# Expert work in one clump behind a slot's own pieces, and token sums that begin two pieces later

## The chip, the cores and the metric

The kernel runs on one core of one Trainium2 chip. The metric is the device time of the slowest core, here the only one, in microseconds. Engines are named as in the profile: PE is TensorE (PEld its weight loads), DVE is VectorE, ACT is ScalarE, POOL is GpSimd, SP issues DMAs. Three runs of the kernel before took 2274.03, 2276.77 and 2281.79 us.

## The reference

Three stages follow each other, all in float32:

```
for t in range(768):                                  # 4 batches x 8 heads, state 48x48
    y[t]  = q[t] @ state
    state = state + beta[t] * outer(k[t], v[t] - k[t] @ state)   # k normalised
x = y as 3072 tokens x 384
P = exp(x @ w_gate); 8 rounds of row and column scaling           # 3072 x 8
x = sum over 8 experts of P[:, e] * (relu(x @ w1[e]) @ w2[e])      # 384 -> 1024 -> 384
out = gelu_sigmoid(x @ w_in) @ w_out                               # 384 -> 2048 -> 384
```

## The kernel before

**Two phases.** First the recurrence runs chunk by chunk, and beside it, on the same engines, the first of the eight experts (`expert0`), the gates and the conversion of the finished tokens. Then come 72 units: 56 for experts 1 to 7 (28 pairs of an expert and a quarter of its hidden columns, for each half of the tokens) and 16 for the MLP. Each unit forms 15 products of sums of token blocks with sums of weight blocks (a fast matrix multiplication, `SCHEME`), turns them into hidden values `h`, and multiplies those by the second weights (`po`).

**The recurrence.** 24 chunks (`u`) of 64 time steps. `Attention.chain` does a chunk in four steps, one matmul group each: `ks` (what the state holds for the keys), `up` (the solved update), `sp` (the new state), `y` (the output). ks is taken from PSUM by DVE (`r`, L356), and up waits for r. Each step yields, and the main loop (L731 to L750) then calls `slot`, so there are 96 slots. What stands in a slot is issued behind that step, and every engine works in the order of issue.

**A slot's own pieces.** `Attention.prep` prepares four chunks at a time (a group), cut into pieces that yield 1.0 or 0.5. The tables `PIECES` and `FIRST` (L29, L32) say how many of them each of a group's 16 slots takes. In order they are: eight gram pieces (`gram`: 16 matmuls `pg` in the trace, which DVE takes from PSUM in three instructions, `am` L187 and twice `x` L200; beside them POOL squares keys, DVE sums the squares, `ss` L127, and works out the step weights in eight small instructions, L141 to L149, and POOL makes the masks `bm`, L167, that the next grams' evictions read); two copies; a transposition on DVE; 30 substitution steps of two DVE instructions each (`lt` L276, `ln` L280), every one of which needs the one before; a transposition `ta` on DVE (L298); and products of 32-row blocks (`pz`, `px`, 64 matmuls each in the trace) with copies by ACT and one more transposition (`tt`, L324). Slots 0 to 2 of a group hold the grams (4, 2, 2), slots 5 to 12 the substitution, slots 13 to 15 the products.

**Expert items.** `expert0` yields after three matmuls: a third of a hidden block (`ph`, 128x256, three such items make one block, which ACT and then DVE take as `h`, L627 and L628) or half a second product (`po`, 128x384). `slot` spreads them: `expert(n / (k + 1) * step)` ahead of each piece and `expert(n / (k + 1))` behind the last, with n about 4.7 items a slot from slot 10 on.

**Turned tokens and gates.** At the second slot of a chunk (behind up), one expert item is issued and then the chunk before is transposed (`xt`, three matmuls, L402) and converted by `emit_x`: ACT writes the high part, DVE the low part (`xb`, L477), ACT the copy that goes to memory (L523). Two chunks make the 256 tokens of an `expert0`. Behind sp the gates' logits (`pl`, nine matmuls) are formed, behind y they are turned (`pt`), in even chunks. All this stands ahead of the slot's own pieces.

**PSUM.** pg, pz, px, xt, pl and pt share one pool of two buffers (`psg`); ks, up, sp and y have two of their own, ph two, po two.

**Token sums.** `sums(i, hf)` (L545) loads three token blocks (`braw`, L567, one buffer) and forms 15 sums of them with POOL; `put` splits a sum in a high part (ACT, `bo` L557) and a low part (POOL, L551) and stores both (L562). `sums(1, 0)` and `sums(1, 1)` make the MLP's tokens in units 29 and later and 57 and later, one step of the generator at certain products (L1108). Their first step behind the loads is a `put` of the loaded blocks themselves.

Of the kernel before, what the change touches and what calls it, by code (L numbers as in the profile page):

```python
# [34 lines left out]
LAG = 10  # L35
# [5 lines left out]
class Attention:  # L41
# [129 lines left out]
    def gram(self, u, planes, h0, n, pool=None):  # L171


        nc, x, j, bm = self.nc, self.X[u // 2 % 4], u % 2, self.bm.get(u)
        hs = slice(h0, h0 + n)
        where, tag = pool or (self.psg, "g")
        ps = where.tile([128, n, len(planes), 64], F32, tag=tag, name="pg")
        for h in range(n):
            for b in range(2):
                dr = slice(64 * b, 64 * b + D)  # L180
                nc.tensor.matmul(
                    ps[64 * (1 - b):64 * (1 - b) + 64, h], x[dr, 0, j, h0 + h],
                    x[dr, planes[0] * (1 + b):planes[-1] * (1 + b) + 1:1 + b, j, h0 + h], start=True, stop=True)
        m = 8 * (u % 4) + h0

        def take():
            nc.vector.tensor_tensor(out=self.am[:, m:m + n], in0=ps[:, :, 0], in1=self.bm[u][:, hs], op=ALU.mult)  # L187

        if pool in self.early:
            return take  # L190
        if planes[0] == 0:
            take()
        if planes[-1] == 1:
            for b in range(2):
                p = slice(64 * (1 - b), 64 * (1 - b) + 64)
                m = x[p, 1 + b, j, hs]
                if u < 8:
                    nc.scalar.copy(out=m, in_=ps[p, :, len(planes) - 1])
                else:
                    nc.vector.tensor_tensor(out=m, in0=ps[p, :, len(planes) - 1], in1=bm[p, hs], op=ALU.mult)  # L200
# [7 lines left out]
    def prep(self, g):  # L208

        nc, am, tt = self.nc, self.am, self.tt  # L210
        w, u = 2 * g, 4 * g
# [60 lines left out]
        for jj in range(1, 31):  # L272
# [16 lines left out]
            if jj == (15 if g == 0 else 22) and g < NG - 1:  # L289
                step = self.weights(*((2, 3) if g == 0 else (w + 2,)))  # L290
# [10 lines left out]
        zs = ta  # L301

        def pz(m0, n):
            ps = self.psg.tile([128, n, 32], F32, tag="g", name="pz")
            for m in range(n):
                for q in (0, 64):
                    nc.tensor.matmul(ps[q + 32:q + 64, m], am[q:q + 32, m0 + m, 32:64],
                                     ta[q:q + 32, m0 + m], start=True, stop=True, tile_position=(q, q + 32))
            for q in (0, 64):
                nc.scalar.copy(out=zs[q + 32:q + 64, m0:m0 + n], in_=ps[q + 32:q + 64])  # L310

        def px(m0, n):
            ps = self.psg.tile([128, n, 32], F32, tag="g", name="px")
            for m in range(n):
                for q in (0, 64):
                    nc.tensor.matmul(ps[q:q + 32, m], zs[q + 32:q + 64, m0 + m],
                                     tt[q + 32:q + 64, m0 + m, 32:64], start=True, stop=True,
                                     tile_position=(q + 32, q))
            for q in (0, 64):
                nc.scalar.copy(out=tt[q:q + 32, m0:m0 + n, 32:64], in_=ps[q:q + 32])  # L320
# [121 lines left out]
def kernel(  # L442
# [32 lines left out]
    def split(dst_hi, dst_lo, src, eng=nc.vector):  # L475
        nc.scalar.copy(out=dst_hi, in_=src)  # L476
        eng.tensor_tensor(out=dst_lo, in0=src, in1=dst_hi.bitcast(F32), op=ALU.subtract)  # L477
# [12 lines left out]
    A = Attention(tc, actx, ident, X, kq, kw, vw, bu, psg)  # L490
# [39 lines left out]
    def emit_x(u, xt):  # L530
        n, c = u // 2, 128 * (u % 2)
        if u % 2 == 0:
            xb[n] = ep.tile([128, 2, 3, 256], F32R, tag="xb", name="xb")
        t = xb[n]
        split(t[:, 0, :, c:c + 128], t[:, 1, :, c:c + 128], xt)
        keep(0, u, xt, ep.tile([128, 3, 128], F32, tag="x32", name="x32"))()
        if u % 2 == 1:
            r = n % 6
            nc.sync.dma_start(
                out=xd[n // 6][r // 2, :, :, :, 256 * (r % 2):256 * (r % 2) + 256].bitcast(F32), in_=xb[n].bitcast(F32))  # L540
# [4 lines left out]
    def sums(i, hf):  # L545


        g = nc.gpsimd

        def tt(o, a, b, op):  # L550
            g.tensor_tensor(out=o, in0=a, in1=b, op=op)  # L551

        def put(at, src):

            n = src.shape[1]
            o = bp.tile([128, 2, 3, 128], F32R, tag="o", name="bo", bufs=2)
            nc.scalar.copy(out=o[:, 0, 0:n], in_=src)  # L557
            yield
            tt(o[:, 1, 0:n], src, o[:, 0, 0:n].bitcast(F32), ALU.subtract)
            yield  # L560
            for k in range(n):
                nc.sync.dma_start(out=xs[i][hf][at + k, :, :, c:c + 128].bitcast(F32), in_=o[:, :, k].bitcast(F32))  # L562

        for c in range(0, 512, 128):
            raw = bp.tile([128, 3, 3, 128], F32, tag="raw", name="braw")
            for t in range(3):
                nc.sync.dma_start(out=raw[:, t], in_=xf[i][hf][t, :, :, c:c + 128])  # L567
            b = [[raw[:, t, d] for t in range(3)] for d in range(3)]
            v = bp.tile([128, 8, 128], F32, tag="v", name="bv")
            yield  # L570
            if i:
                yield from put(8, raw[:, 0:3, 0])
            tt(v[:, 4], b[2][1], b[2][2], ALU.subtract)
            tt(v[:, 5], b[0][0], b[1][0], ALU.add)
            tt(v[:, 0], b[1][2], v[:, 4], ALU.add)
            tt(v[:, 1], v[:, 4], b[0][2], ALU.subtract)
            yield
            if i:
                yield from put(11, raw[:, 1:3, 1])
            tt(v[:, 2], v[:, 5], b[1][1], ALU.subtract)  # L580
            tt(v[:, 3], v[:, 2], v[:, 1], ALU.subtract)
            tt(v[:, 3], v[:, 3], b[0][1], ALU.subtract)
            yield from put(0, v[:, 0:2])
            tt(v[:, 4], b[1][2], v[:, 5], ALU.subtract)
            tt(v[:, 5], b[1][1], b[1][0], ALU.subtract)
            tt(v[:, 5], v[:, 5], b[2][0], ALU.add)
            yield from put(2, v[:, 2:4])
            tt(v[:, 6], b[0][2], b[2][0], ALU.subtract)
            tt(v[:, 6], v[:, 6], b[2][2], ALU.add)
            tt(v[:, 7], zero, b[1][2], ALU.subtract)  # L590
            tt(v[:, 7], v[:, 7], b[2][0], ALU.subtract)
            yield from put(4, v[:, 4:6])
            if i:
                yield from put(13, raw[:, 0:2, 2])
            yield from put(6, v[:, 6:8])
            yield
# [94 lines left out]
    ex = []  # L691

    def expert_item():
        while ex:
            if next(ex[0], None) is not None:
                return True
            ex.pop(0)
        return False

    prep = chain.from_iterable(A.prep(g) for g in range(NG))  # L700
# [7 lines left out]
    done, due = 0, 0.0  # L708

    def expert(n):  # L710

        nonlocal done, due
        due += n
        while done < due and expert_item():
            done += 1

    def slot(t):

        n, k = rate * ITEMS[t % 16] if t >= LAG else 0, (PIECES if t > 15 else FIRST)[t % 16]
        if t == LAG:  # L720
            expert(BURST)
        i = 0
        while i < k:
            expert(n / (k + 1) * step[0])
            step[0] = next(prep, 1.0)
            i += step[0]
        expert(n / (k + 1))

    step = [1.0]
    build = sums(0, 0)  # L730
    for u in range(NU):  # L731
        for s, _ in enumerate(A.chain(u)):
            if s == 1 and u > 0:
                if 4 * u >= LAG:
                    due -= 1
                    expert(1)
                    done += expert_item()
                while u % 2 == 1 and len(ex) > 1:
                    done += expert_item()
                emit_x(u - 1, A.xt())  # L740
                if u % 2 == 0:
                    ex.append(expert0(u // 2 - 1))
            if s > 1 and u > 0 and u % 2 == 0:
                (logits if s == 2 else turn)(u // 2 - 1)
            slot(4 * u + s)
            while A.ready < u // 4:
                next(prep)
            next(ew, None)
            if u > 12:
                next(build, None)  # L750
        if u % 2 == 1 and u // 2 + 4 < 12:
            A.load_k(u // 2 + 4)
            A.load_x(u // 2 + 4)
# [300 lines left out]

    conv = convert64()
    building = [sums(0, 1)]
    later, turns = [], []
    load_w2(0)
# [8 lines left out]
    for j in range(len(units) + 1):  # L1067
# [3 lines left out]
        for k in range(len(SCHEME)):  # L1071
# [20 lines left out]
            if turns and turns[0][0] <= now:  # L1092
                u = turns.pop(0)[1]
# [75 lines left out]
```

## Time and profile before

| | |
|---|---|
| median of 3 runs | 2276.77 us |
| profiled execution: its time, its span | 2275.14 us, 2273.4 us |
| mean granted TensorE clock | 0.974 |
| busy: PE, DVE, ACT, POOL | 95%, 67%, 47%, 50% |
| start of the recurrence's last y (L389) in the span | 503.45 us |

The profile is one execution. Times in rows are microseconds from the span's start. A timeline row gives start, duration, engine, line, operation, tile written and tiles read, shape and count, and in brackets how long the engine was idle before and what ended it. A row of the waits gives who waited for whom, the total, how often, and the longest. A row of the stretches gives for each engine busy microseconds and instructions, then the granted clock (1.00 is 2.4 GHz, 0.50 is 1.2 GHz) and the DMAs' share and rate. Matmul ends are modelled, so lengths of matmul work are read from start to start.

### The profile page before, as it was taken

The numbers are of one execution on the slowest core, as the hardware profiler recorded it, in microseconds if no ns is written. First come the engines' busy times: TensorE is split into PE (matmuls) and PEld (weight loads), VectorE is DVE, ScalarE is ACT, GpSimd is POOL, SyncE is SP. The second block draws the span as 40 slices with busy tenths as digits, with TensorE's granted clock in tenths as the row PEclk, the third lists the DMA queues.
The fourth block names the chain that finished last, engine by engine and source line by source line (L and its number), as shares of the span: only waits on it lengthen the run. The fifth ranks groups of instructions, "written<-read, shape, count | busy, mean of one in ns | idle before, by whom it ended". The sixth has DMA issues, their size and how long they took to land. (4 is left out here: it accounts for less than half of the span.)

```text
span 2273.4 us, 40807 instructions
## 1 busy us (share of the span) xinstructions
PE 2161.1 (95%) x15663; PEld 1945.2 (86%) x15663; DVE 1520.3 (67%) x2754; ACT 1065.2 (47%) x2125; POOL 1128.3 (50%) x1326
## 2 busy tenths in 40 slices
PE   4499999998999999999999999999999999999999
PEld 4488888896989999999998989998989998888988
DVE  6666866626766677776666767777765556666675
ACT  2334344444444444444445444454554446555554
POOL 5511132224677766666652655565655334752333
PEclk8599999999999999999999999999999999999999
DMA  5223334238435343333358656556455366557231
GB/s 120 61 82 82 88 97 115 76 103 314 143 114 181 122 166 132 128 126 122 143 198 251 185 166 193 175 178 217 160 180 163 113 231 177 159 157 247 91 118 49
DMA packets 229155, 336.74 MB, mean 148 GB/s; under 512 B 15649, under 2 KB 192417, under 8 KB 224801
## 3 DMA queue, kind: packets, MB, share of 16 engines
q1 hardware_dynamic: 228240, 333.26, 45.6%
q8 instruction: 123, 2.02, 0.4%
q10 hardware_dynamic: 720, 0.89, 0.1%
q14 instruction: 72, 0.58, 0.1%
HBM read 204.58 MB, written 129.50 MB: 147 GB/s over the span
## 5 line engine op out<-in xcount | busy, mean ns | idle before, releaser
L481 PE MATMUL po<-w2c,h 128*128 128x384 f32 x1728 | 588.2, 340 | 0.0
L482 PE MATMUL po<-w2c,h 128*128 128x384 f32 x1728 | 586.4, 339 | 0.7 <-DVE h L982 0.7
L480 PE MATMUL po<-w2c,h 128*128 128x384 f32 x1728 | 580.1, 336 | 0.3 <-ACT h L980 0.2
L480 PE MATMUL c<-xt,w1c 128*128 128x512 f32 x1080 | 431.3, 399 | 19.8 <-DVE sg L979 10.5
L1037 POOL TENSOR_TENSOR acc<-acc,ye 128x384 f32<-128x384 f32 x252 | 263.0, 1044 | 374.9 <-ACT ye L1036 357.4
L482 PE MATMUL c<-xt,w1c 128*128 128x512 f32 x1080 | 430.6, 399 | 2.3 <-POOL w1c L477 2.3
L481 PE MATMUL c<-xt,w1c 128*128 128x512 f32 x1080 | 429.3, 398 | 0.0
L1014 DVE TENSOR_TENSOR o<-o,c 128x512 f32<-128x512 f32 x288 | 197.5, 686 | 255.9 <-PE c L482 232.1
L1039 DVE SCALAR_TENSOR_TENSOR acc<-po,P,acc 128x384 f32<-128x384 f32 x420 | 258.3, 615 | 153.0 <-PE po L482 150.5
L480 PEld LDWEIGHTS po<-w2c,h 128*128 128x128 f32 x1728 | 325.7, 188 | 40.3 <-ACT ye L1036 0.7
L481 PEld LDWEIGHTS po<-w2c,h 128*128 128x128 f32 x1728 | 324.7, 188 | 40.0
L482 PEld LDWEIGHTS po<-w2c,h 128*128 128x128 f32 x1728 | 325.8, 189 | 1.1 <-DVE h L982 1.1
L1036 ACT ACTIVATE ye<-po,P 128x384 f32<-128x384 f32 x252 | 146.9, 583 | 349.9 <-PE po L482 336.1
L480 PEld LDWEIGHTS c<-xt,w1c 128*128 128x128 f32 x1080 | 203.8, 189 | 50.9 <-DVE h L973 19.6
L482 PEld LDWEIGHTS c<-xt,w1c 128*128 128x128 f32 x1080 | 203.3, 188 | 47.8 <-POOL w1c L477 3.1
L481 PEld LDWEIGHTS c<-xt,w1c 128*128 128x128 f32 x1080 | 203.7, 189 | 9.0
L1007 ACT COPY o<-c 128x512 f32<-128x512 f32 x288 | 163.9, 590 | 56.5 <-PE c L482 55.4
L971 ACT ACTIVATE h<-c 128x512 fp32r<-128x512 f32 x168 | 96.7, 599 | 175.2 <-DVE c L1014 168.0
L1049 POOL TENSOR_TENSOR acc<-acc,ye 128x384 f32<-128x384 f32 x84 | 92.6, 1103 | 165.6 <-ACT ye L1048 160.1
L477 POOL TENSOR_TENSOR w2c<-w2r,w2c 128x384 fp32r<-128x384 f32 x140 | 147.1, 1051 | 34.8 <-ACT w2c L476 34.8
L1014 DVE TENSOR_TENSOR f<-o,c 128x512 f32<-128x512 f32 x216 | 149.2, 691 | 12.7 <-PE c L482 3.3
L971 ACT ACTIVATE h<-f 128x512 fp32r<-128x512 f32 x168 | 100.4, 598 | 72.8 <-DVE f L1014 70.6
(175 smaller groups left out, 3545.0 us busy)
## 6 DMA issues: line engine op xcount, KB each, us to landing
w1c<-wd SPq DMA_DIRECT2D x210, 384.0 KB, 4.4
wd<-w1c SPq DMA_DIRECT2D x28, 1920.0 KB, 7.0
xs<-bo SPq DMA_DIRECT2D x184, 128.0 KB, 2.2
xt<-xs SPq DMA_DIRECT2D x46, 512.0 KB, 6.0
w2r<-in_w_dram SPq DMA_DIRECT2D x55, 384.0 KB, 5.9
wd<-wo SPq DMA_DIRECT2D x56, 256.0 KB, 3.1
w1r<-in_w_dram SPq DMA_DIRECT2D x28, 384.0 KB, 7.6
x<-in_kq_dram SPq DMA_DIRECT2D x24, 384.0 KB, 6.5
```

Source lines behind the costliest of these rows:

```text
L477: eng.tensor_tensor(out=dst_lo, in0=src, in1=dst_hi.bitcast(F32), op=ALU.subtract)
L480: nc.tensor.matmul(ps, lhs[0], rhs[0], start=start, stop=False, **kw)
L481: nc.tensor.matmul(ps, lhs[0], rhs[1], start=False, stop=False, **kw)
L482: nc.tensor.matmul(ps, lhs[1], rhs[0], start=False, stop=stop, **kw)
L971: nc.scalar.activation(out=h[:, 0], in_=src, func=ACTF.Relu)
L1007: nc.scalar.copy(out=o, in_=ps)
L1014: nc.vector.tensor_tensor(out=d, in0=o, in1=ps, op=ALU.add if how == "add" else ALU.subtract)
L1036: nc.scalar.mul(ye, ps, P[:, u, e:e + 1])
L1037: nc.gpsimd.tensor_tensor(out=a, in0=a, in1=ye, op=ALU.add)
L1039: nc.vector.scalar_tensor_tensor(out=a, in0=ps, scalar=P[:, u, e:e + 1], in1=a, op0=ALU.mult, op1=ALU.add)
L1049: nc.gpsimd.tensor_tensor(out=a, in0=a, in1=ye, op=ALU.add)
```

## The change

`slot` now issues the slot's own pieces first. `A.small` marks pieces that hold matmuls (gram, pz, px); behind each second one, if another piece follows, half of the slot's expert items are put in. Then come the turned tokens, gates or turned gates (`turned`), then the remaining expert items. The one expert item that was forced ahead of a transposition is gone. In `sums`, for the MLP's tokens, the first `put` comes two steps of the generator later, so each of four blocks of a half takes two more steps.

```diff
@@ -172,6 +172,7 @@
 
 
         nc, x, j, bm = self.nc, self.X[u // 2 % 4], u % 2, self.bm.get(u)
+        self.small = True
         hs = slice(h0, h0 + n)
         where, tag = pool or (self.psg, "g")
         ps = where.tile([128, n, len(planes), 64], F32, tag=tag, name="pg")
@@ -301,6 +302,7 @@
         zs = ta
 
         def pz(m0, n):
+            self.small = True
             ps = self.psg.tile([128, n, 32], F32, tag="g", name="pz")
             for m in range(n):
                 for q in (0, 64):
@@ -310,6 +312,7 @@
                 nc.scalar.copy(out=zs[q + 32:q + 64, m0:m0 + n], in_=ps[q + 32:q + 64])
 
         def px(m0, n):
+            self.small = True
             ps = self.psg.tile([128, n, 32], F32, tag="g", name="px")
             for m in range(n):
                 for q in (0, 64):
@@ -569,6 +572,8 @@
             v = bp.tile([128, 8, 128], F32, tag="v", name="bv")
             yield
             if i:
+                yield
+                yield
                 yield from put(8, raw[:, 0:3, 0])
             tt(v[:, 4], b[2][1], b[2][2], ALU.subtract)
             tt(v[:, 5], b[0][0], b[1][0], ALU.add)
@@ -714,35 +719,39 @@
         while done < due and expert_item():
             done += 1
 
-    def slot(t):
+    def slot(t, turned):
+
 
         n, k = rate * ITEMS[t % 16] if t >= LAG else 0, (PIECES if t > 15 else FIRST)[t % 16]
         if t == LAG:
             expert(BURST)
-        i = 0
+        i = m = 0
         while i < k:
-            expert(n / (k + 1) * step[0])
-            step[0] = next(prep, 1.0)
-            i += step[0]
-        expert(n / (k + 1))
-
-    step = [1.0]
+            A.small = False
+            i += next(prep, 1.0)
+            m += A.small
+            if m == 2 and i + 1 < k:
+                expert(n / 2)
+                n, m = n / 2, 0
+        turned()
+        expert(n)
+
+    def turned(u, s):
+
+        nonlocal done
+        if s == 1 and u > 0:
+            while u % 2 == 1 and len(ex) > 1:
+                done += expert_item()
+            emit_x(u - 1, A.xt())
+            if u % 2 == 0:
+                ex.append(expert0(u // 2 - 1))
+        if s > 1 and u > 0 and u % 2 == 0:
+            (logits if s == 2 else turn)(u // 2 - 1)
+
     build = sums(0, 0)
     for u in range(NU):
         for s, _ in enumerate(A.chain(u)):
-            if s == 1 and u > 0:
-                if 4 * u >= LAG:
-                    due -= 1
-                    expert(1)
-                    done += expert_item()
-                while u % 2 == 1 and len(ex) > 1:
-                    done += expert_item()
-                emit_x(u - 1, A.xt())
-                if u % 2 == 0:
-                    ex.append(expert0(u // 2 - 1))
-            if s > 1 and u > 0 and u % 2 == 0:
-                (logits if s == 2 else turn)(u // 2 - 1)
-            slot(4 * u + s)
+            slot(4 * u + s, lambda: turned(u, s))
             while A.ready < u // 4:
                 next(prep)
             next(ew, None)
```

Three places show what moved. In the second slot of chunk 8 (behind `up`), on TensorE: pg is a gram piece, xt the transposition of the chunk before, po and ph are expert items. Before:

```order
L402 MATMUL xt<-ident,ys 128x128 x3
L480 MATMUL po<-w2s_202,h 128x384
L481 MATMUL po<-w2s_202,h 128x384
L482 MATMUL po<-w2s_202,h 128x384
L181 MATMUL pg<-x_128 64x128 x8
L480 MATMUL po<-w2s_202,h 128x384
L481 MATMUL po<-w2s_202,h 128x384
L482 MATMUL po<-w2s_202,h 128x384
L181 MATMUL pg<-x_128 64x128 x8
L480 MATMUL ph<-xb,w1s_187 128x256
```

Now, from `up` on:

```order
L368 MATMUL up<-r,tt 64x48 x16
L182 MATMUL pg<-x_128 64x128 x16
L405 MATMUL xt<-ident,ys 128x128 x3
L483 MATMUL po<-w2s_202,h 128x384
L484 MATMUL po<-w2s_202,h 128x384
L485 MATMUL po<-w2s_202,h 128x384
```

Both grams now stand next to up and ahead of xt, with no expert item between them.

The same place on VectorE, from the last of the eight weight instructions (wt) on; am and x take a gram from PSUM, xb takes the turned tokens, S is the new state. Before:

```order
L149 TENSOR_TENSOR wt<-wt,nr 128x16
L477 TENSOR_TENSOR xb<-xt,xb 128x3x128
L187 TENSOR_TENSOR am<-pg,bm 128x256
L200 TENSOR_TENSOR x_128<-pg,bm 64x256 x2
L187 TENSOR_TENSOR am<-pg,bm 128x256
L200 TENSOR_TENSOR x_128<-pg,bm 64x256 x2
L382 TENSOR_TENSOR S<-S,sp 112x384
```

Now:

```order
L149 TENSOR_TENSOR wt<-wt,nr 128x16
L188 TENSOR_TENSOR am<-pg,bm 128x256
L201 TENSOR_TENSOR x_128<-pg,bm 64x256 x2
L188 TENSOR_TENSOR am<-pg,bm 128x256
L201 TENSOR_TENSOR x_128<-pg,bm 64x256 x2
L480 TENSOR_TENSOR xb<-xt,xb 128x3x128
L633 SCALAR_TENSOR_TENSOR h<-ph,h 128x256
L385 TENSOR_TENSOR S<-S,sp 112x384
```

The tokens' low part moved behind the evictions of both grams.

On ScalarE at the first block of the sums of unit 29: bo from braw is the first `put`, h, o, ye and w2c are the unit's own evictions and weight splits. Before:

```order
L1036 ACTIVATE ye<-po,P 128x384
L920 ACTIVATE acc<-acc,P 128x384
L557 CAST bo<-braw 128x384
L1009 ACTIVATE o<-c_13900 128x512
L476 CAST w2c<-w2r 128x384
L1007 COPY o<-c_14065 128x512
```

Now:

```order
L1045 ACTIVATE ye<-po,P 128x384
L929 ACTIVATE acc<-acc,P 128x384
L1018 ACTIVATE o<-c_13900 128x512
L479 CAST w2c<-w2r 128x384
L1016 COPY o<-c_14062 128x512
L1045 ACTIVATE ye<-po,P 128x384
L560 CAST bo<-braw 128x384
```

Four of the unit's own instructions moved ahead of the put.

## Rows read from the trace of the kernel before

**Rows 1.** The page: busy time of the engines, share of the span, instructions.

```profile
PE 2161.1 (95%) x15663; PEld 1945.2 (86%) x15663; DVE 1520.3 (67%) x2754; ACT 1065.2 (47%) x2125; POOL 1128.3 (50%) x1326
```

**Rows 2.** Stretches (PE, PEld, DVE, ACT, POOL busy; granted clock; DMA).

```profile
224.00:245.00 21.00, 21.00 (x284) 17.15 (x281) 14.85 (x39) 5.00 (x12) 5.85 (x5) 1.00 0.27 87
245.00:282.00 37.00, 35.64 (x500) 32.21 (x497) 30.75 (x91) 15.35 (x34) 2.76 (x3) 1.00 0.34 87
...
435.03:445.27 10.24, 10.24 (x119) 9.42 (x119) 2.12 (x3) 4.20 (x7) 0.00 (x0) 0.50 0.17 46
...
1336.15:1339.57 3.42, 3.42 (x11) 3.06 (x10) 0.48 (x1) 1.66 (x5) 3.05 (x7) 0.50 0.50 136
```

**Rows 3.** Waits between 100 and 520 us.

```profile
PE up L365 <- DVE r L356: 10.0, 4, 5.6
...
PE pz L307 <- DVE ta L298: 4.3, 5, 1.6
```

**Rows 4.** Timeline of TensorE, grams of chunk 8: ph and po between grams.

```profile
225.88 0.39 PE L480 MATMUL ph<-xb,w1s 128*128 128x256 f32 x1
...
226.43 1.09 PE L181 MATMUL pg<-x 48*64 48x128 f32 x16
...
227.44 0.44 PE L480 MATMUL po<-w2s,h 128*128 128x384 f32 x1
...
228.17 1.09 PE L181 MATMUL pg<-x 48*64 48x128 f32 x16
...
241.54 0.39 PE L480 MATMUL ph<-xb,w1s 128*128 128x256 f32 x1
...
242.45 1.09 PE L181 MATMUL pg<-x 48*64 48x128 f32 x16
```

**Rows 5.** Timeline of VectorE, grams of chunk 8.

```profile
225.99 0.42 DVE L187 TENSOR_TENSOR am<-pg,bm 128x256 f32<-128x256 f32 x1 [0.94 <-PE pg L181]
226.43 0.86 DVE L200 TENSOR_TENSOR x<-pg,bm 64x256 f32<-64x256 f32 x2
...
230.53 0.94 DVE L127 TENSOR_REDUCE ss<-sq 128x16 f32<-128x768 f32 x1
...
232.59 0.15 DVE L141 TENSOR_SCALAR nr<-ns 128x16 f32<-128x16 f32 x1
...
235.53 0.42 DVE L187 TENSOR_TENSOR am<-pg,bm 128x256 f32<-128x256 f32 x1 [0.58 <-POOL bm L167]
```

**Rows 6.** Timeline of VectorE, second slots of chunks 2 and 9.

```profile
112.54 0.39 DVE L276 TENSOR_TENSOR lt<-ln 128x234 f32<-128x234 f32 x1
...
116.05 0.56 DVE L477 TENSOR_TENSOR xb<-xt,xb 128x384 fp32r<-128x384 f32 x1
...
253.58 0.56 DVE L477 TENSOR_TENSOR xb<-xt,xb 128x384 fp32r<-128x384 f32 x1 [0.52 <-ACT xb L476]
```

**Rows 7.** Timeline of TensorE, chunk 2's third slot and chunk 11's second.

```profile
117.36 0.38 PE L480 MATMUL pl<-xb,wgs 128*8 128x256 f32 x1
...
280.57 1.13 PE L365 MATMUL up<-r,tt 64*64 64x48 f32 x32
...
283.56 1.20 PE L307 MATMUL pz<-ta,am 32*32 32x32 f32 x64 [0.81 <-DVE ta L298]
```

**Rows 8.** Timeline of ScalarE at two puts of the MLP's token sums.

```profile
1330.28 0.51 ACT L557 CAST bo<-braw 128x384 fp32r<-128x384 f32 x1 [6.79 <-DMA braw<-xf]
...
1960.70 0.51 ACT L557 CAST bo<-braw 128x384 fp32r<-128x384 f32 x1 [3.93 <-DMA braw<-xf]
```

**Rows 9.** Timeline of SP at the first of these, and of TensorE behind both.

```profile
1323.26 1.90 SPq L567 DMA_DIRECT2D braw<-xf  x3
...
1335.62 0.50 PE L480 MATMUL c<-xt,w1c 128*128 128x512 f32 x1 [2.98 <-DVE h L973]
...
1964.30 0.80 PE L480 MATMUL c<-xt,w1c 128*128 128x512 f32 x1 [3.89 <-DVE sg L979]
```

**Rows 10.** Waits between 1850 and 2050 us.

```profile
ACT bo L557 <- DMA xs<-bo: 12.8, 8, 4.4
```

## The prediction

> **What bounds the kernel now.** I read the page's busy times first: TensorE is busy 95% of the span [rows 1], so time is won where it waits, or where its work gets shorter. Next the stretches of the recurrence [rows 2]. With grams in the slots (224 to 245 us) TensorE is busy all 21.00 us and VectorE 14.85. In the substitution steps (245 to 282) VectorE is busy 30.75 of 37.00 us, and TensorE loses 1.36 us. Both engines are near their limit there, and the waits name the places [rows 3]: up waits 10.0 us for r (5.6 of it once, before any expert item is issued), pz 4.3 us for the transposition ta. After the recurrence the units keep TensorE busy except at a few places, two of which hang on a put of the token sums [rows 8, 9].
>
> **The change part by part.**
>
> *Boundaries between small and whole-array matmuls.* Three ph between two grams take 0.55 us from start to start (225.88 to 226.43), six take 0.91 (241.54 to 242.45) [rows 4]. Three ph alone are the difference, 0.36, so a return trip between grams and expert work costs 0.19 us, a boundary 0.095. Along TensorE's whole order up to the last y there are 272 such boundaries before and 178 now. 94 x 0.095 = 8.9 us less. At the other end the gain is nothing, if TensorE comes earlier only to wait. I take 8.9 and book the waits apart.
>
> By the Trainium skill (TensorEngine Tiling (Array Packing), Key Properties) any change of tiling mode, not of the tile alone, drains the engine. By that, up next to pz and y next to px (64-row beside 32-row pieces, ten new neighbours) would still pay, and the gain is 84 x 0.095 = 8.0 us; no run here shows such neighbours at the full clock.
>
> *The transposition behind grams.* xt now stands behind both grams of its slot, and with two buffers it needs the one that the slot's first gram filled. VectorE takes a gram in 0.42 + 0.86 = 1.3 us [rows 5], TensorE makes one in 1.0 (226.43 to 227.44 [rows 4]). Count from the end of ks in chunk 8. VectorE: first eviction from 1.1 on, second done at 3.7; the third gram is ready at 4.6 (two grams, 1.5 us of items, one gram), taken at 5.9; the sum of squares 0.94, so 6.8; the fourth 8.1; the eight weight instructions and the wait for the mask 2.9 (232.59 to 235.53), so 11.0; the fifth 12.3. TensorE: four grams 4.0; items of six ph and twelve po, 0.72 + 4 x 0.54 (three po between grams take 227.44 to 228.17, 0.73, less 0.19), and two return trips, 3.3 in all; up 1.1 [rows 7]; two grams 2.0: it reaches xt at 10.4. It waits 1.9 us. There are four such slots (chunks 4, 8, 12, 16): +7.6. The ends: 0, if evictions keep up as they do now, and 3.5 each (14), if hidden blocks or the mask come between.
>
> *Gates behind grams.* pl, behind sp, needs the buffer of the first of two grams: 1.1 + 1.3 = 2.4 us after sp against 2.0 on TensorE. 4 x 0.4 = +1.6; 0 to 3.
>
> *Tokens behind substitution steps.* In the second slot of chunks 2, 6, 10, 14 and 18 VectorE now runs eight step instructions ahead of xb; eight of them took from 112.54 to 116.05, 3.5 us [rows 6]. In chunk 2 xb would end at 116.05 + 3.5 + 0.56 = 120.1, and TensorE could use it from 117.36 on [rows 7]: +2.7. In chunk 6 new expert work also stands right behind xt, with three po as cover: I take +2.0, the nearest case being chunk 2. In the others the tokens are first read behind sp, whose 1.1 us and the slot's items cover most. Together +4.7; 1 to 9.
>
> *An earlier start of the steps.* In chunk 9 the steps stood behind xb and a wait for it, 0.56 + 0.52 us [rows 6], and the transposition ahead of them stood behind an h, which is now issued after it. I take 1.5 us of head start; in four groups 6.0 of the 8.7 us of waits that are left (10.0 - 5.6 + 4.3 [rows 3]). Against it: pz follows up at once, where an expert item and xt stood between. In chunk 11 up starts at 280.57 and takes 1.1, and TensorE waits only the last 0.81 ahead of 283.56 [rows 7]: 1.1 us of cover there, 0.8 I take for the five such slots, 4.0. Net -2.0; between -8.7 and +5.
>
> *The clock.* From 435.03 to 445.27, behind the longest wait for ta (1.6), TensorE ran at a granted clock of 0.50 [rows 2, 3]: 10.24 us that would have taken half, 5.1 lost. New waits of about 2 us can bring falls, old waits that shrink can take this one away. I take them as even: 0, between -5.1 and +20.
>
> Recurrence: -8.9 + 7.6 + 1.6 + 4.7 - 2.0 + 0 = +3.0 us.
>
> *Token sums.* The loads of a block begin at 1323.26 [rows 9], ScalarE reaches the put at 1323.5 and stands still 6.79 us [rows 8]. It is served in order, so the evictions behind it wait, and TensorE stops 2.98 us; then it runs 3.42 us at 0.50 (1336.15 to 1339.57), 1.7 lost. The second such place: 3.93 us of ScalarE, 3.89 of TensorE and, at the same price, 1.7. Together 10.3 us. Two steps later is about 5 us in units 29 on (three steps in five products; a unit is at most (2273.4 - 503.45) / 72 = 24.6 us, so a product 1.6) and 3.3 in units 57 on. That leaves ScalarE 1.8 and 0.6 us to wait. At the first place 6.79 of its wait became 2.98 of TensorE's, so 1.8 is covered; at the second nearly all of it came through, so 0.6 stays. -9.7; from -13 to 0, since the later steps of each block also shift against the units, and ScalarE waits 12.8 us in all for stores of the same two buffers [rows 10]. The extra steps themselves issue nothing. The loads stay where they are, one buffer, behind the block before.
>
> Sum: the profiled execution took 2275.14 us, a span of 2273.4 and 1.7 around it. 2275.1 + 3.0 - 9.7 = 2268.4, so **2268 us**. The profiled execution stands 1.6 below the median of the three runs, 2276.77, and well inside their spread of 7.8, so I add nothing for it.
>
> **The rivals.**
>
> *The clump is free.* The evictions keep up, no new wait shows, and the old fall at 435 goes: 2275.1 - 8.9 - 9.7 - 5.1 = 2251, with some tokens late 2254. For it: VectorE has 6 us free in 21 with grams. Against it: those gaps lie where it waits for TensorE, and its list above has no gap but one of 0.9.
>
> *The clump costs more than it saves.* The waits behind grams are 3.5 each, and tokens come late in five chunks (9): -8.9 + 14 + 3 + 9 - 2.0 = +15, less 9.7: 2280. Between that and the forecast lies "no change".
>
> *The sums only move their waits.* The put waits no more, but other puts and stores now fall on the units' evictions, with the same 10 us: 2275.1 + 3.0 = 2278. For it: ScalarE's 12.8 us of waits for stores [rows 10]; against it: those lie in the time before already, and a block with two more steps leaves the stores more room.
>
> *The other side: the clock.* The new wait at xt lies between grams, and in three or four gram stretches the clock falls and stays low for 10 us, as at 435: 4 x 5.1 = 20.4: 2268.4 + 20.4 = 2289, slower by 0.5%. It decides from three falls of that length on. For it: the only long fall so far lies among small matmuls. Against it: grams ran at the full clock in all of 224 to 245 [rows 2].
>
> **How the numbers follow.** A measurement of this kernel can tell about 0.3%, 6.8 us, from no change: the bounds are 2269.9 and 2283.6. The forecast gets 0.48 (its own range 2261 to 2275, six in ten of it faster), the free clump 0.20, the costly clump 0.12, the moved waits 0.10 and the clock 0.10. Faster: 0.29 + 0.20 + 0.02 = 0.51. Slower: 0.09 of the clock and 0.03 of the costly clump: 0.12. Same: 0.37. The range reaches from 2254, half of the free clump, to 2282, which leaves out the clock.
>
> **What the profile would show.** Right: about 9 us less TensorE time up to the last y where nothing waits; xt waiting about 2 us in chunks 4, 8, 12 and 16, released by VectorE's eviction of a gram; pl or ph waiting for xb in chunks 2 and 6; shorter waits of up for r; no stop near 1335 and 1964, and no wait of ScalarE's first put over 2 us. Wrong: a last y that is over 6 us earlier or 10 us later than 503.45, long stretches at 0.50 among the grams, or stops of TensorE over 2 us in the units with token sums.

## The result, and the profile after

The changed kernel takes 2290.93 us (median of six runs, 2286.69 to 2297.03), the kernel before on the same chip 2275.40 (six runs, 2271.58 to 2281.79). The ratio is 1.0065, with a 95% interval of 1.0049 to 1.0081: slower, by about 15 us. The forecast was 2268, faster, with a range up to 2282.

The profiled execution took 2290.1 us, a span of 2288.3, 14.9 more than before. The page's busy line, which answers to [rows 1]:

```profile
PE 2152.7 (94%) x15663; PEld 1945.0 (85%) x15663; DVE 1524.6 (67%) x2754; ACT 1061.5 (46%) x2125; POOL 1128.4 (49%) x1326
```

TensorE is busy 8.4 us less, so what was added is time in which it stands still. The last y ends at 525.38 us, 20.8 later than before (504.58). Behind it the span is 5.9 us shorter. The stretch from 100 us to the last y, of before and then of after (columns as in [rows 2]):

```profile
100.00:504.58 404.58, 383.75 (x5999) 341.57 (x5996) 254.00 (x647) 166.11 (x352) 91.40 (x114) 0.96 0.35 93
```

```profile
100.00:525.38 425.38, 379.20 (x6007) 345.40 (x6007) 256.35 (x647) 164.86 (x353) 91.42 (x114) 0.94 0.33 89
```

TensorE's idle time grows from 20.8 to 46.2 us, and the granted clock falls from 0.96 to 0.94. The waits between 100 and 530 us say for what it stands still; they answer to [rows 3]:

```profile
PE xt L405 <- DVE x L201: 10.8, 4, 2.9
PE up L368 <- DVE r L359: 8.8, 3, 6.0
PE ph L484 <- DVE xb L480: 6.5, 3, 4.3
PE pl L484 <- DVE xb L480: 6.1, 3, 2.4
PE ph L483 <- DVE h L633: 3.5, 4, 1.4
PE pl L483 <- DVE x L201: 2.7, 4, 0.7
PE pz L309 <- DVE ta L299: 2.5, 5, 0.6
```

Four of these rows are the turned tokens and the gates in their new places. xt waits for a gram's buffer (10.8 us, four times). ph and pl wait for the low part xb (12.6 us, six times; before 0.8). pl waits for a gram's buffer (2.7, four times). The trace shows how it happens at two kinds of place. The first is chunk 8. TensorE's and VectorE's timelines there, which answer to [rows 4, 5]:

```profile
242.77 1.70 PE L182 MATMUL pg<-x 48*64 48x128 f32 x28
246.88 0.88 PE L405 MATMUL xt<-ident,ys 128*128 128x128 f32 x3 [2.42 <-DVE x L201]
```

```profile
242.51 0.16 DVE L141 TENSOR_SCALAR nr<-ns 128x16 f32<-128x16 f32 x1
...
244.11 0.17 DVE L149 TENSOR_TENSOR wt<-wt,nr 128x16 f32<-128x16 f32 x1
245.44 0.42 DVE L188 TENSOR_TENSOR am<-pg,bm 128x256 f32<-128x256 f32 x1 [1.16 <-POOL bm L167]
245.88 0.86 DVE L201 TENSOR_TENSOR x<-pg,bm 64x256 f32<-64x256 f32 x2
```

TensorE has finished the slot's two grams and reaches xt at 244.46. VectorE has then just ended the eight small instructions, waits 1.16 us for POOL's mask, and takes the first gram until 246.7. Before, the same wait of VectorE for the mask was there too (0.58, [rows 5]), but TensorE had xt and expert items to do meanwhile. The other three such places, in chunks 4, 12 and 16, have waits of 2.94, 2.83 and 2.60 us.

The second place is chunk 6, where the slot's pieces are substitution steps:

```profile
196.42 0.55 PE L405 MATMUL xt<-ident,ys 128*128 128x128 f32 x3
...
202.59 0.58 PE L484 MATMUL ph<-xb,w1s 128*128 128x256 f32 x1 [4.28 <-DVE xb L480]
```

```profile
196.86 0.41 DVE L277 TENSOR_TENSOR lt<-ln 128x240 f32<-128x240 f32 x1
...
201.68 0.39 DVE L281 TENSOR_TENSOR ln<-ln,lt 128x220 f32<-128x220 f32 x1
201.98 0.55 DVE L480 TENSOR_TENSOR xb<-xt,xb 128x384 fp32r<-128x384 f32 x1
```

xt is done by 197, but from there on twelve step instructions still stand ahead of xb on VectorE, and the next hidden block needs xb.

All six falls of the granted clock between 125 us and the last y begin in one of these waits or within 1.7 us behind its end:

```profile
164.53:167.94 3.41, 3.34 (x15) 3.34 (x16) 0.44 (x2) 0.86 (x2) 0.78 (x1) 0.50 0.50 154
202.07:208.90 6.83, 6.31 (x52) 5.33 (x53) 3.17 (x7) 1.41 (x5) 0.00 (x0) 0.50 0.69 210
246.45:249.86 3.41, 2.98 (x11) 3.01 (x12) 2.02 (x5) 1.44 (x4) 2.82 (x2) 0.50 0.00 0
321.54:324.95 3.41, 3.41 (x13) 3.41 (x12) 1.40 (x3) 0.96 (x2) 2.19 (x2) 0.50 0.01 4
362.50:369.32 6.82, 5.75 (x23) 5.15 (x23) 5.78 (x17) 2.50 (x7) 0.10 (x1) 0.50 0.48 155
403.46:410.29 6.83, 5.87 (x50) 5.46 (x52) 2.96 (x7) 1.54 (x4) 6.67 (x10) 0.50 0.32 100
```

Behind the recurrence the token sums do what they were forecast to do at one of the two places. The stop at the first block [rows 8, 9] is gone: TensorE is busy all of both stretches around the same place, now some 21 us later, at the full clock. At the second place a shorter stop is left, 2.46 us instead of 3.89, and the clock falls behind it as before (0.50 for 3.41 us from 1983.83 on):

```profile
1337.00:1350.00 13.00, 13.00 (x66) 11.66 (x65) 9.78 (x16) 6.27 (x14) 8.06 (x11) 1.00 0.65 193
1350.00:1363.00 13.00, 13.00 (x67) 11.74 (x67) 10.21 (x17) 6.24 (x13) 6.48 (x7) 1.00 0.77 235
```

```profile
1983.51 0.54 PE L483 MATMUL c<-xt,w1c 128*128 128x512 f32 x1 [2.46 <-DVE sg L988]
```

ScalarE's wait for loads at the puts (6.79 and 3.93 us in [rows 8]) is 2.1 us in all, once. Its waits for stores [rows 10] are 15.0 us where they were 12.8. Both as rows between 1865 and 2065 us:

```profile
ACT bo L560 <- DMA xs<-bo: 15.0, 9, 3.0
ACT bo L560 <- DMA braw<-xf: 2.1, 1, 2.1
```

### The profile page after: what moved, and what is told of

It is laid out like the page before. It is cut to its first block, busy times and chain, and to the rows that moved or that the text cites. A ratio compares the mean times of both kernels' runs of the same rounds, so it can differ in the third digit from the quotient of the medians.

```text
span 2288.3 us, 40800 instructions
## 1 busy us (share of the span) xinstructions
PE 2152.7 (94%) x15663; PEld 1945.0 (85%) x15663; DVE 1524.6 (67%) x2754; ACT 1061.5 (46%) x2125; POOL 1128.4 (49%) x1326
## 4 chain that ended last, share of the span: by engine, by line
PE 74%; DVE 13%; POOL 4%; issue 3%; ACT 3%; DMA 2%; SPq 1%; POOLq 0%; ACTq 0%; DVEq 0%
PE po L485 12%; PE po L484 12%; PE po L483 12%; PE c L483 10%; PE c L484 9%; PE c L485 9%; DVE lt L277 3%; DVE ln L281 3%; PE ph L483 1%; PE ph L484 1%; PE ph L485 1%; PE pg L182 1%; PE y L392 1%; POOL bv L554 1%; PE sp L379 1%
## 5 line engine op out<-in xcount | busy, mean ns | idle before, releaser
L1023 DVE TENSOR_TENSOR f<-o,c 128x512 f32<-128x512 f32 x216 | 148.9, 689 | 12.6 <-PE c L485 3.5
```

Of the source, the lines that this page charges most:

```text
L1023: nc.vector.tensor_tensor(out=d, in0=o, in1=ps, op=ALU.add if how == "add" else ALU.subtract)
```

## The experiments

Two theories. **A, tokens:** the loss comes from the turned tokens and gates standing behind a slot's own pieces. **B, clump:** it comes from the expert items no longer standing between the pieces. Each kernel below was timed in three rounds against the kernel before; the ratios have 95% intervals. They reach 2 to 5 us to either side, so differences of a few microseconds between two of these kernels are not shown. Where an expectation names the last y, it means its start (503.45 before, 524.25 after); elsewhere its end is given, 1.1 us later.

### The tokens first again

```diff
 # the changed kernel
     def slot(t, turned):
...
+        turned()
         if t == LAG:
             expert(BURST)
...
-        turned()
         expert(n)
```

> The changed kernel, with the turned tokens and the gates put back to the start of a slot, ahead of its own pieces; the clump of expert items behind the pieces and the later sums stay. Theory A, tokens: the recurrence ends 20.8 us later because the transposition xt and the gates now stand behind grams and substitution steps. Its waits in the trace after are xt for DVE x 10.8, ph and pl for DVE xb 12.6, and 30.7 us at clock 0.50 in the recurrence against 13.65 before, about 8.5 us of work. Then the last y falls from 524 to about 500, the sums keep their -10, and the time is 2257 to 2266; the waits of ph and pl for xb are below 2 us. Theory B, clump: the loss comes from expert items that no longer stand between the pieces as cover for evictions. Then tokens first change little: 2282 to 2291, the last y at 518 or later.

2273.57 us, ratio 0.9994 (0.9975 to 1.0014): 17 us less than the changed kernel. A holds for the loss. But it isn't the 2257 to 2266 of A either: the last y ends at 510.7, 6.1 later than before. So something that is left in this kernel has a cost of its own, the clump or the missing extra item (tested apart below). Its waits:

```profile
PE ph L483 <- DVE h L633: 10.0, 7, 3.1
PE up L368 <- DVE r L359: 8.7, 3, 5.7
PE pg L182 <- ACT x L526: 5.3, 4, 1.7
```

xt and xb are gone from the list (0.9 us of xb is left). In their place hidden blocks wait for VectorE's h and grams for ScalarE. At 355.19 a ph waits 3.14 us for h, which stands on VectorE behind steps of the substitution:

```profile
355.19 0.58 PE L483 MATMUL ph<-xb,w1s 128*128 128x256 f32 x1 [3.14 <-DVE h L633]
```

```profile
354.45 0.25 DVE L281 TENSOR_TENSOR ln<-ln,lt 128x84 f32<-128x84 f32 x1
...
354.78 0.69 DVE L633 SCALAR_TENSOR_TENSOR h<-ph,h 128x256 fp32r<-128x256 f32 x2
```

### The later sums alone

```diff
 # the kernel before
             if i:
+                yield
+                yield
                 yield from put(8, raw[:, 0:3, 0])
```

> The kernel before, with nothing changed but the token sums, begun two pieces later. Both theories: the two stages behind the recurrence gained 10.2 us together in the trace after, and this part touches nothing else: 2263 to 2268, the last y at 503 as before. If only the shift of the recurrence made the sums faster (the transfers they wait for being then earlier against them), it is 2273 to 2277.

2266.38 us, ratio 0.9955 (0.9934 to 0.9976): 10.4 us faster, as expected. Its profiled execution has a span 9.7 us shorter than before. The last y ends at 501.28, 3.3 earlier than before, in an execution that has no fall of the clock at 435; the change does not touch that stage. The other 6.4 us lie behind the recurrence. The interval (5 to 15 us) holds both sizes.

### The tokens late, alone

```diff
 # the kernel before; turned() holds xt, gates and turned gates, without the extra item
             expert(n / (k + 1) * step[0])
             step[0] = next(prep, 1.0)
             i += step[0]
+        turned()
         expert(n / (k + 1))
...
```

> The kernel before, with nothing changed but the turned tokens and the gates, put behind the slot's own pieces; the expert items stay spread between the pieces and the sums begin where they did. Theory A, tokens: this alone costs the recurrence about 20 us: 2290 to 2300, last y at 520 to 526, with waits of xt for DVE x near 10 us and of ph and pl for xb near 12 us. Theory B, clump: 2273 to 2281, last y below 510.

2299.81 us (four runs), ratio 1.0113 (1.0089 to 1.0137), last y 528.3 (its start, 527.2, is 1.2 beyond the expected range). A is right, and the tokens' place needs no clump to cost 23 us. The waits are smaller than expected, the clock falls are longer:

```profile
PE ph L481 <- DVE xb L477: 7.6, 4, 3.4
PE xt L402 <- DVE x L200: 4.5, 3, 2.6
```

```profile
233.80:244.00 10.20, 10.20 (x79) 8.40 (x78) 3.30 (x8) 2.41 (x5) 1.47 (x1) 0.50 0.04 7
244.00:254.28 10.28, 10.28 (x77) 8.35 (x76) 5.07 (x16) 1.16 (x3) 1.96 (x2) 0.50 0.01 2
```

For 20.5 us TensorE is busy without a gap and gets half the clock. What it does there is grams, ks and up with a few whole-array matmuls between. Ahead of it stand px and a gap of 0.51 us, no long wait.

### The transposition in another PSUM pool

```diff
 # the changed kernel
-        xt = self.psg.tile([128, 3, 128], F32, tag="g", name="xt")
+        xt = self.psc.tile([128, 3, 128], F32, tag="c", name="xt")
```

> The changed kernel, with the transposition xt taking its PSUM buffer from the chain's pool and not from that of the grams. Theory A in its first half (xt waits until an eviction of a gram frees its buffer: 10.8 us of waits of xt for DVE x, with falls of the clock behind them): those waits shrink to below 3 us, the last y moves from 524 to about 512, and the time is 2278 to 2283. If the waits for xb behind the substitution steps (12.6 us) carry the loss, the time stays within 2287 to 2291. Theory B: no change, 2289 to 2292, or slower where the chain then waits for its own buffer.

2281.25 us, ratio 1.0022 (1.0005 to 1.0039): 9.7 us less than the changed kernel. The last y ends at 516.4, in a profiled execution that is the fastest of the ten (2275.72); its start, 515.2, is 3 later than expected. The waits of xt are gone. Part of them came back one step later: xb stands behind the grams' evictions on VectorE too, and ph's waits for xb grew from 6.5 to 11.5 us, while pl's fell from 6.1 to 2.9.

```profile
PE ph L484 <- DVE xb L480: 11.5, 4, 4.3
PE up L368 <- DVE r L359: 6.7, 3, 4.0
PE ph L483 <- DVE h L633: 5.7, 4, 2.6
PE pl L483 <- DVE x L201: 4.1, 4, 2.1
PE pl L484 <- DVE xb L480: 2.9, 3, 1.6
```

### Transposition or gates

```diff
 # the changed kernel: gates late, xt first (the other kernel: s > 1 here, s == 1 below)
+            if s == 1:
+                turned(u, s)
-            slot(4 * u + s, lambda: turned(u, s))
+            slot(4 * u + s, lambda: s > 1 and turned(u, s))
```

> The changed kernel, with only the transposition xt (and the tokens xb that follow from it) back at the start of its slot; the gates (pl and pt) stay behind the slot's own pieces. With both moved back the time was 2273.6, with both behind 2290.9. If it is xt's place that costs (it waits for a gram's eviction, and xb, which ph and pl wait for, comes that much later), the loss goes almost wholly: 2273 to 2278, last y 510 to 514, no wait of ph or pl for xb over 1.5 us. If the gates' place carries a half: 2280 to 2284.

> The reverse: the changed kernel with only the gates back at the start of their slots, and xt behind the slot's pieces. If xt's place costs, the loss stays: 2285 to 2293, last y 518 to 528, with waits of xt for DVE x near 10 us and of ph and pl for xb near 12 us. If the gates' place carries a half: 2279 to 2284.

Gates late: 2274.93 us, ratio 0.9996 (0.9981 to 1.0011). That is 1.4 above the kernel with both first, which is within the noise; pl waits 2.7 us for a gram's buffer. xt late: 2286.86, ratio 1.0050 (1.0032 to 1.0068), 13.3 above. xt's place carries the loss.

### xt late among grams, or among steps

```diff
 # the changed kernel (the other kernel: u % 4 > 0)
+            late = s == 1 and u % 4 == 0
+            if not late:
+                turned(u, s)
-            slot(4 * u + s, lambda: turned(u, s))
+            slot(4 * u + s, lambda: late and turned(u, s))
```

> The changed kernel with the gates first, and xt behind the slot's pieces only in chunks 4, 8, 12, 16 and 20, whose pieces there are grams (up to 16); elsewhere xt comes first. None late is 2273.6, all late 2286.9. By the waits (xt for DVE x 10.8 us, four of 2.4 to 2.9, each followed by a fall to clock 0.50): 2280 to 2286. If the waits of ph for xb behind the substitution steps are what the lateness costs: 2274 to 2278.

> The reverse: xt behind the slot's pieces in every chunk but 4, 8, 12, 16 and 20; where the pieces are substitution steps, xb then stands behind them on VectorE. The waits of ph and pl for xb at these places in the trace after are 1.98 (chunk 2), 4.28 (chunk 6) and 1.5 to 2.4 behind chunks 10, 14 and 18, with one fall of 6.8 us at chunk 6: 2279 to 2284. If the waits of xt behind the grams are what the lateness costs: 2274 to 2278.

Among grams: 2284.74 us, ratio 1.0029 (1.0020 to 1.0039), 11.2 above the kernel with the tokens first; xt's four waits are again 10.8 us. Elsewhere: 2281.80, ratio 1.0020 (1.0009 to 1.0032), 8.2 above; the waits for xb are 9.4 us (ph 4.3, pl 5.1). So both halves of A cost. Whether their costs add up is not shown: by the medians they are 11.2 and 8.2 us against 13.3 for both, by the ratios 8.0 and 5.9 against 12.7, and each has an uncertainty of several microseconds.

### The extra item

```diff
 # the kernel with the later sums alone
-                if 4 * u >= LAG:
-                    due -= 1
-                    expert(1)
-                    done += expert_item()
```

> The kernel with the later sums alone (2266.4), less one thing that the change also removes: the expert item that is issued ahead of its turn before each transposition xt, as cover between up and pz. The clump with the tokens first was 7.2 us slower than the later sums alone. If this item is what the clump loses, 2271 to 2275, with longer waits of pz for ta and of pl or ph behind xt. If the clump itself loses it (ph waits 10.0 us for VectorE's h, pg 5.3 us for ScalarE), 2263 to 2269.

2265.01 us, ratio 0.9948 (0.9931 to 0.9965): not to be told from 2266.38. With the items spread, the item ahead of xt shows no price; so it is the clump that loses what the kernel with the tokens first lost.

### The clump in the first chunks only

```diff
 # the kernel with the tokens first; spread and extra item as before from chunk 10 on
         i = m = 0
+        while t >= 40 and i < k:
+            expert(n / (k + 1) * step[0])
+            step[0] = next(prep, 1.0)
+            i += step[0]
+        if t >= 40:
+            n /= k + 1
         while i < k:
...
```

> Tokens first and later sums; the clump only in chunks 0 to 9, and from chunk 10 on the expert items spread between the pieces, with the extra item before xt. With the clump throughout, the end of y was 2.6 us earlier than before at chunk 9 and 6.1 later at the last, that is 8.7 lost from chunk 10 on; with the sums alone it was 1.0 later at chunk 9. If the clump's loss lies where it shows, the last y is at 498 to 502 and the time 2261 to 2266, the fastest so far. If the later chunks pay for what the earlier ones put off, the last y is at 504 or more and the time 2268 to 2274.

2260.87 us (2259.9 to 2268.11), ratio 0.9946 (0.9926 to 0.9966). The profiled execution is a long one of these, with a span of 2266.4; its last y starts at 502.2 and ends at 503.3. The time fits the first account (0.1 below its range), the last y misses it by 0.2. This kernel and the two before it here (later sums alone, and without the extra item) beat both the kernel before and the changed one; their intervals don't tell them apart.

### The clump ahead of the pieces

```diff
 # the kernel with the tokens first
-        i = m = 0
+        i = 0
+        expert(n)
         while i < k:
-            A.small = False
             i += next(prep, 1.0)
-            m += A.small
-            if m == 2 and i + 1 < k:
-                expert(n / 2)
-                n, m = n / 2, 0
-        expert(n)
```

> Tokens first and later sums, with the clump throughout but ahead of the slot's pieces and not behind them. Tokens first with the clump behind the pieces was 2273.6, the sums alone 2266.4. Theory: the clump's own cost is that its evictions stand on VectorE behind the step instructions of the pieces (ph waits 10.0 us for VectorE's h, 1.7 before). Then those waits fall below 4 us, the last y comes to 504 or earlier, and the time is 2264 to 2269. Rival: the cost is that pieces and items each come in a row, whichever is first, and evictions pile up behind either: 2271 to 2277, with grams or pz waiting for ScalarE and VectorE instead.

2274.53 us, ratio 0.9991 (0.9976 to 1.0006). The waits of ph for h fell from 10.0 to 2.9 us as the theory said, and the time stayed: the theory is wrong, and the rival has the time right. The waits that the rival named, of grams and pz, did not grow against the kernel with the tokens first; what grew is up's wait for r, from 8.7 to 19.8 us:

```profile
PE up L368 <- DVE r L359: 19.8, 8, 5.8
PE ph L484 <- DVE xb L480: 3.4, 3, 1.4
PE ph L483 <- DVE h L633: 2.9, 2, 2.6
```

At the longest of the new ones, ahead of 418.76, r stands on VectorE behind sixteen step instructions and an h. The steps are those of the slots before, which now come behind their items:

```profile
411.37 0.29 DVE L277 TENSOR_TENSOR lt<-ln 128x130 f32<-128x130 f32 x1
...
417.75 0.40 DVE L281 TENSOR_TENSOR ln<-ln,lt 128x228 f32<-128x228 f32 x1
418.06 0.55 DVE L359 TENSOR_TENSOR r<-ks,v 128x384 f32<-128x384 f32 x1
```

```profile
418.76 1.17 PE L368 MATMUL up<-r,tt 64*64 64x48 f32 x32 [3.82 <-DVE r L359]
```

So with the clump behind the pieces h stands behind the steps, and with the clump ahead of them r does. Both are read from single places; that this backlog of steps is the whole cost of the clump is not shown.

## Why the prediction was wrong

What the recurrence gained and lost can be added up from the matmul records between 100 us and the last y: TensorE's idle time, its busy time inside the stretches at clock 0.50, and its work, which is the busy time with that part taken half. Half is an estimate: neighbouring po start 0.175 us apart at the full clock and 0.32 at 0.50 in the trace before, 1.83 times as far. The boundaries are those between small and whole-array matmuls (ph, po, xt, pl and pt) in the same records.

| kernel | last y ends | idle | busy at 0.50 | work | boundaries |
|---|---|---|---|---|---|
| before | 504.6 | 20.8 | 27.1 | 370.2 | 271 |
| later sums alone | 501.3 | 22.2 | 15.8 | 371.1 | 271 |
| clump in the first chunks | 503.3 | 23.4 | 28.6 | 365.7 | 239 |
| clump, tokens first | 510.7 | 32.1 | 32.0 | 362.6 | 203 |
| clump ahead, tokens first | 509.8 | 35.9 | 39.4 | 354.2 | 171 |
| changed kernel | 525.4 | 46.2 | 42.8 | 357.8 | 177 |
| tokens late alone | 528.3 | 31.3 | 53.2 | 370.3 | 267 |

From before to after: idle +25.4, work -12.4, half the busy time at the lower clock +7.9. That is +20.9, the lateness of the last y. (With 1.83 in place of 2 the last two are -11.7 and +7.1.) The forecast had +3.0: its waits, 7.6 + 1.6 + 4.7 - 2.0, came to +11.9 where TensorE's idle time grew by 25.4, its boundaries to -8.9, its clock to 0. So the waits were 13.5 us too low and the clock 7.9, and the boundaries gave back 3.5.

- **Boundaries, -8.9: right in kind, too small.** The work fell by 12.4 us with 94 boundaries less, 0.13 each; over the kernels with fewer boundaries it is 0.11 (tokens first) to 0.16 (clump ahead), where 0.095 was read from two places among grams. That reading goes from the first ph to the next gram and leaves out the way from a gram to the ph. In the trace after, two neighbouring grams take 1.90 us up to the po behind them (238.09 to 239.99); in the trace before a gram alone takes 1.02 (228.17 to 229.19). The second gram adds only 0.88, so leaving a gram for expert work costs 0.14 more than going on to the next gram. For ks it is 0.10: 0.97 up to a pg behind it, 1.07 up to a po. A return trip is then 0.29 to 0.33 us and not 0.19, an estimate from these rows. The Trainium skill (TensorEngine Tiling (Array Packing), Key Properties) says that changing the tiling mode drains TensorE; by that, the ten new small neighbours save nothing. The trace after agrees for the five where y stands next to px: y takes 1.07 us up to px, as it does up to a po. At the five where up stands next to pz, pz waits for ta and nothing can be read.
- **The transposition behind grams, +7.6: the mechanism right, the size low.** xt waits in just the four chunks named, 10.8 us, 2.7 each instead of 1.9. VectorE's list was the one foretold; its wait for the mask is 1.07 us on average (0.82 to 1.16) and not 0.58. These four waits, 4.3 us, are part of the 10.8; no kernel with earlier masks was run. The bound of 14 held it. In time, xt late among grams cost 11.2 us by the medians, 8.0 by the ratios.
- **Gates behind grams, +1.6: within its range.** pl waits 2.7 us, where it had no such wait before; the 1.4 us in time are within the noise.
- **Tokens behind substitution steps, +4.7: this step failed, in its last sentence.** Chunk 2 waits 1.98 us (2.7 forecast) and chunk 6 4.28 (2.0). The three chunks called covered by sp and the slot's items (10, 14, 18) wait 1.54, 2.08 and 2.45: pl stands right behind sp, ahead of its slot's items, and what lies between xt and pl, sp and the items of xt's own slot, is used up before xb is done. Together 12.3 us of waits, above the upper bound of 9; xt late outside the gram slots cost 8.2 us in time by the medians, 5.9 by the ratios.
- **An earlier start of the steps, -2.0: as far as it shows, right.** up's waits for r fell from 10.0 to 8.8 us and pz's for ta from 4.3 to 2.5 [rows 3], 3.0 less in all.
- **The clock, 0: this step failed too.** The old fall at 435 is gone, as the step allowed, but six falls came, each at one of the new waits: 7.9 us net, inside the range of the step. The new waits were priced at their own length, where the falls put about a third on top (7.9 on 25.4 us of idle time). "Even" was the wrong value beside ten forecast new waits.
- **The clump's waits behind its own evictions: missing from the sum.** The forecast costed the clump's boundaries and not that three to five items in a row wait for evictions of their own that stand behind steps on VectorE. The kernel with the tokens first shows its net price: 11.3 us more idle time and 2.5 more lost to the clock against 7.6 less work, and a time 7.2 us above the later sums alone. With the tokens late too this adds little (the later sums and late tokens, added, make 2289.4, and the changed kernel is 2290.9).
- **Token sums, -9.7: right in size, wrong at the second place.** Alone they gave 10.4 us (5 to 15). Behind the last y the eleven traces with the later sums are 1757.5 to 1764.3 us long, 1761.0 on average, and the two without 1768.8 and 1772.7. But of the second stop 0.6 us was to stay, and 2.46 and its fall of the clock did: this sign of being wrong came true, and so did that of the last y, 20.8 us later.

Of the rivals, the one on the other side gave the nearest time, 2289, but not by its own mechanism. It wanted three falls that stay for 10 us among grams. In the changed kernel four of the six falls do stand at xt's waits, but the six last 3.4 to 6.8 us, and most of what it lost is waiting. That its number is near is luck. A long fall among grams, of 20.5 us, did come in the kernel with the tokens late alone.

Still open is why clumps that stand behind and ahead of the pieces end at the same time, and whether the clump in the first chunks gains anything on the sums alone. Of the first, the traces show longer waits behind VectorE's steps in both; an order of items without them was not found.

## What to carry to other kernels

When instructions are put behind others on every engine, list for each of them what its buffer and its input now stand behind on the evicting engine, and give each such place a price, also those that seem covered; check the cover by its order, since work issued behind the waiting instruction covers nothing. On a kernel whose main engine loses its clock after a wait, price a new wait above its length. A change with two independent halves should be split: here the ten microseconds of the later sums were there to be had all the time, and the other half cost 25.

## What the runs showed of the hardware

- The same short gap stood ahead of a fall of the clock in one execution and of none in another, a difference of about 5 us by estimate (half of 10.24). In the kernel without the extra item TensorE waits 0.95 us at 158.28, and from 160.45 on the clock is 0.50 for 10.24 us; the kernel before has the same gap (0.96, at 158.72) and the full clock behind it. The two stretches, of the kernel without the item and then of the kernel before, hold 82 and 143 matmuls:

```profile
160.45:170.69 10.24, 10.24 (x82) 8.15 (x80) 3.73 (x9) 1.13 (x3) 4.45 (x4) 0.50 0.45 136
```

```profile
160.45:170.69 10.24, 10.24 (x143) 8.48 (x141) 6.46 (x16) 1.52 (x4) 4.89 (x4) 1.00 0.45 136
```

- In the long falls (10.2 us at 435 before, 10.2 at 160 here, 20.5 at 234 with the tokens late alone) TensorE has no gap, and groups of small matmuls (pg, ks, up, sp, pz) alternate with whole-array ones.
- The 65 executions of the kernel before that were timed beside the experiments took 2268.31 to 2285.17 us, and they go with the mean granted clock: the 13 at 0.971 or 0.972 took 2279.3 to 2285.2, the 15 at 0.977 and above 2268.3 to 2279.4. So one profiled execution can't tell two kernels apart that lie within 10 us.
